# A decode block whose 26 large loads are issued by GpSimd in place of the sync engine

## The chip, the cores and the metric

The kernel runs on one core of a Trainium2 chip. A core has a matrix engine (TensorE, PE in the profile, its weight loads PEld), a vector engine (VectorE, DVE), a scalar engine (ScalarE, ACT), a general engine (GpSimd, POOL) and a sync engine (SyncE, SP). Each runs its own list of instructions in order and waits on semaphores for the others. Data come from memory by DMA: an engine issues a load, and 16 DMA engines carry it. In this kernel SP and ACT issue loads. The metric is device time in microseconds, the median of several runs.

## The reference

One decode step of a transformer block for a batch of 2 with one token each, hidden size 512. All is float32.

```
mod = silu(c) @ w_mod                        # 512 x 3072, cut into sa, ca, ga, sb, cb, gb
h   = layernorm(x) * (1 + ca) + sa
x   = x + ga * attention(h)                  # 32 query heads, 8 key heads, head size 128
h   = layernorm(x) * (1 + cb) + sb
x   = x + gb * (silu(h @ w1) @ w2)           # 512 x 1792 and back
```

The attention computes `q = h @ wq`, takes the last 4096 keys and values of the caches for each of the two tokens and the 8 key heads, and ends with `@ wo`. The caches' windows are 67 MB of the 97.5 MB that have to be read; w_mod, wq, wo, w1 and w2 are the rest. Every byte is used once.

## The kernel before

**The ring.** All large loads go into one buffer, `slots`, of 8 slots of 16 KB a partition. `stream(n)` hands out the next n slots in turn. `load_pair` (L77) loads the keys or the values of two heads of one token, 4096 KB, into two slots; `load_runs` (L88) loads a weight or a part of one. These two functions issue all 26 large loads, in program order: w_mod (three slots), wq (four slots), then for the eight steps of the attention K of the next step and V of the last one (16 loads), wo in two parts, w1 in two, w2 in four. A load into a slot waits until what stood there has been used. K of step 0 and K of step 1 take slots 0 to 3 after w_mod; V of step 0 takes slots 4 and 5 after wq.

**The start.** c is fetched by four small loads that ACT issues (L105), x by one that SP issues (L109). POOL makes the constants: a zeroed square and a diagonal (`ident`), then, from it by DVE, `id4` (L116) and other sums over `ident`, and from those on POOL `rep4` (L125), `selh`, `quad` (four selects, L185), `mix`, `selg`, a row of small memsets, and the memsets of `qg` and `qbd` (L210), `oTn` (L214), `hT` (L292) and `uT` (L293). DVE turns c (`cT`, L255) and, with ACT, makes silu of it (`scT`, L261). PE multiplies `scT` with w_mod in four rounds of four matmuls each into `m_a` (two of the six parts of mod, L269) and `m_sp` (the other four, L272). For the layer norm of x two small matmuls average statistics (`mean_a`, L236; `var_a`, L245); ACT takes a square root (L247). From `m_a` and the normalised x come `h_a` and its turned form `hq_T`. ACT copies `m_sp` to `mod_sp` (L286); one is added to one part of it (L287); three parts are turned (`gaT`, `sbT`, `cbT`, L255).

**The query.** PE computes q (L302) from wq and `hq_T`. `place(n)` spreads each half: DVE turns it (L315), four copies of 32 partitions bring it into `qg` (L319), a matmul with `rep4` repeats it (L323), four copies make `qbd` (L329). `place(0)` stands before the attention, `place(1)` in its third step.

**The attention.** In each of eight steps DVE turns the keys (`keys`, L361, eight transposes of 128 x 1024), PE computes scores (L374), DVE and PE find maxima, ACT takes the exponentials (L406), the result is turned and spread (`turn`, L418 to L435), and PE multiplies by the values (`weighted`, L448). Then come wo, the second layer norm, w1, silu and w2; `busy(n)` adds matmuls whose result is not used. The output is stored by a DMA from SP (L704).

**Order.** Inside the attention and behind it most instructions are kept in program order by hand (`inorder`). In the start they are not: the framework's scheduler orders each engine's list, by when it estimates that an instruction can run. Where an instruction moves to another engine, or a load to another queue, the lists of the start can come out in another order, also for instructions that the diff does not touch.

Of the kernel before, what the change touches and what calls it, by code (L numbers as in the profile page):

```python
# [10 lines left out]
ALU = mybir.AluOpType  # L11
# [12 lines left out]
def adaln_block(  # L24
# [19 lines left out]
    nc = tc.nc  # L44
# [16 lines left out]
    def const(shape, name):  # L61
        return consts.tile(shape, F32, name=name)

    def bank(tag, name):
        return (psum1 if tag in "CO" else psum).tile([P, 512], F32, tag=tag, name=name)
# [4 lines left out]
    def stream(n=1):  # L70
        i = turn_of[0]
        if n % 2 == 0:
            i += -i % n
        turn_of[0] = i + n
        return slots[:, i % RING : i % RING + n, :].rearrange("p s e -> p (s e)")

    def load_pair(cache, s):  # L77


        i, b = divmod(s, B)  # L80
        t = stream(2)
        nc.sync.dma_start(
            t,
            cache[b, 2 * i : 2 * i + 2, SK - W :, :].rearrange("e (u n) d -> u e (n d)", u=P // 2),
        )
        return t

    def load_runs(w, per, lo, hi):  # L88

        e = w.shape[1]  # L90
        n = -(-(hi - lo) * e // 4096)
        t = stream(n)[:, : (hi - lo) * e].rearrange("p (q e) -> p q e", e=e)
        nc.sync.dma_start(t, w.rearrange("(p q) e -> p q e", q=per)[:, lo:hi, :])
        return t


# [2 lines left out]
    x_sp, c_sp = xc[:, 0, :], xc[:, 1, :]  # L99
    nc.vector.memset(xc, 0.0)  # L100
    wm = load_runs(w_mod, 4, 0, 4)
    rows8 = lambda t: t.rearrange("(ab r) m -> ab r m", r=16)[:, 0, :]
    for b in range(B):
        for lo in (0, 2):
# [3 lines left out]
            )  # L108
    nc.sync.dma_start(rows8(x_sp), x2.rearrange("b (g m) -> g b m", m=P))  # L109
    wqt = load_runs(wq, 4, 0, 4)  # L110


# [103 lines left out]
    mod_sp = const([P, 4, P], "mod_sp")  # L216
# [36 lines left out]
    def turned(t, name):  # L253
        o = const([P, 4, 32], name)
        nc.vector.transpose(o, t.rearrange("p (m k) -> p k m", k=4))  # L255
        return o
# [7 lines left out]
    for k in range(4):  # L264
# [8 lines left out]
        if k == 0:  # L273
# [3 lines left out]
                xn, x_sp, mean_a, rstd_a, op0=ALU.subtract, op1=ALU.mult  # L277
# [6 lines left out]
    nc.vector.tensor_add(h_a, h_a, mod_a[:, 0, :])  # L284
    hq_T = turned(h_a, "hq_T")
    nc.scalar.copy(mod_sp.rearrange("p s m -> p (s m)"), m_sp)  # L286
    nc.gpsimd.tensor_scalar(mod_sp[:, 2, :], mod_sp[:, 2, :], 1.0, None, op0=ALU.add)  # L287
    ga, sb, cb1, gb = (mod_sp[:, s, :] for s in range(4))


    hT, uT = const([P, 4, 32], "hT_b"), const([P, F // P, 32], "uT")
# [18 lines left out]
    inorder = tc.keep_in_program_order  # L310

    def place(n):

        qT = once.tile([P, D], F32, tag="wide", name=f"qT{n}").rearrange("p (s j r) -> p s j r", s=4, r=32)
        inorder(nc.vector.transpose(qT.rearrange("p s j r -> p (s j r)"), q_ps[n]))  # L315
        for g in range(G):
            r = slice(32 * g, 32 * g + 32)
            eng = nc.gpsimd if g % 2 else nc.vector
            inorder(eng.tensor_copy(  # L319
                qg[n][r, :, :, :, g], qT[r, :, :, 0:32:16].rearrange("p s j b -> p s b j")  # L320
            ))
        rp = bank("C", f"qr{n}")[:, :P]
        inorder(nc.tensor.matmul(  # L323
            rp, rep4, qg[n].rearrange("p s b j g -> p (s b j g)"), start=True, stop=True
        ))
        for i in range(4):
            r = slice(32 * i, 32 * i + 32)
            cp = nc.scalar.copy if i % 2 else nc.vector.tensor_copy
            inorder(cp(  # L329
                qbd[n][r].rearrange("p s b j c -> p (s b j) c")[:, :, 4 * i : 4 * i + 4],  # L330
                rp[r, :].rearrange("p (m g) -> p m g", g=G),
            ))

    place(0)


# [12 lines left out]
    def fetch(s):  # L349

        if s < STEPS:
            kt[s] = load_pair(k_cache, s)
        if s > 0:
            vt[s - 1] = load_pair(v_cache, s - 1)
# [122 lines left out]
    for s in range(STEPS + 1):  # L477
        if s < STEPS:
            fetch(s + 1)
            scores(s, 0)  # L480
        if s > 0 and s != STEPS - 1:
            turn(s - 1)
        if s > 1:
            collect(s - 2)
        if s == 2:
            place(1)
        if s < STEPS:
            for j in range(1, 4):
                keys(s, j)
                scores(s, j)  # L490
            maxima(s)
            exponentials(s)
        if s < STEPS - 2:
            keys(s + 1, 0)
        if s > 0:
            weighted(s - 1)
        if s == STEPS - 2:
            turn(s)
            keys(s + 1, 0)
    collect(STEPS - 1)  # L500

    gaT, sbT, cbT = turned(ga, "gaT"), turned(sb, "sbT"), turned(cb1, "cbT")
    nc.gpsimd.tensor_copy(hT[:, :, 1:32:16], sbT[:, :, 0:32:16])
    ax = once.tile([P, P], F32, tag="ax", name="ax")
    for lo, hi in ((0, 24), (24, 32)):
        wt = load_runs(wo, 32, lo, hi)
        wot.extend(wt[:, q, :] for q in range(hi - lo))
# [69 lines left out]
    for q in range(28):  # L577
        g = q % 4
# [68 lines left out]
    for b in range(B):  # L647
# [5 lines left out]
            op0=ALU.mult,  # L653
# [5 lines left out]
    for tt in range(WIDE):  # L659
        g = tt % 4  # L660
# [21 lines left out]
    for tt in range(11, T2):  # L682
        for h in range(2):
            for g in range(4):
                lo = g * P + h * H
# [46 lines left out]
```

## Time and profile before

| | |
|---|---|
| median of 3 runs | 235.51 us (235.45 to 235.78) |
| profiled execution, first to last instruction | 233.7 us |
| PE busy | 161.1 us, 69% |
| DVE busy | 115.6 us, 49% |
| ACT busy | 28.5 us, 12% |
| POOL busy | 10.5 us, 4%, 35 instructions |
| read from memory | 97.53 MB, 417 GB/s over the span |

The profiled execution shows its span, 233.7 us; the time of a run is measured around it, and the median is 1.8 us longer. In the lines of the profile an engine's row reads: start, length, engine, line, operation, output and input, and in brackets how long the engine was idle before and what ended that. SPq and ACTq are the lists from which SP and ACT issue loads; the length of such a row is the issue, not the transfer. A row's `x8` is a number of instructions merged into one row.

### The profile page before, as it was taken

To read this page: it belongs to the slowest core of one execution; us is meant where nothing else is said; L and a number is where in the kernel's file an instruction comes from. 1 tells how busy PE (TensorE), PEld (TensorE's weight loads), DVE (VectorE), ACT (ScalarE), POOL (GpSimd) and SP (SyncE) were. 2 spreads that over 40 slices of the span, in tenths; PEclk is the share of its full clock that TensorE was granted. 3 is DMA by queue.
4 is the path that set the end of the run, shared out by engine and by line. 5 is a ranking of instruction groups with operands and counts; after the bars stand their busy time and mean duration, and the time that the engine had idled before them with its cause. 6 is when DMAs were issued, how large, how long until landed. Compare 5 with 4: busy or idle time off the path is not lost.

```text
span 233.7 us, 2571 instructions
## 1 busy us (share of the span) xinstructions
PE 161.1 (69%) x1070; PEld 43.3 (19%) x1070; DVE 115.6 (49%) x179; ACT 28.5 (12%) x64; POOL 10.5 (4%) x35
## 2 busy tenths in 40 slices
PE   0004916859577839797598749759759779789684
PEld 0001401201111111211120201202112122324222
DVE  0007240278894758695197089259559540101232
ACT  2000210000311120120210201111020120102020
POOL 2004710000000000000000000000000000000000
PEclk9999985979999977999979999988997997999999
DMA  7998998999999999999999999999999999989991
GB/s 269 446 542 359 404 494 359 446 444 421 415 421 449 446 437 415 426 426 446 449 437 409 418 437 449 449 421 412 426 444 449 443 421 437 463 367 437 424 404 57
DMA packets 3794, 97.68 MB, mean 418 GB/s; under 512 B 432, under 2 KB 456, under 8 KB 968
## 3 DMA queue, kind: packets, MB, share of 16 engines
q1 hardware_dynamic: 3768, 97.53, 97.1%
q8 instruction: 8, 0.13, 0.2%
q14 instruction: 2, 0.02, 0.0%
q10 hardware_dynamic: 16, 0.00, 0.0%
HBM read 97.53 MB, written 0.00 MB: 417 GB/s over the span
## 4 chain that ended last, share of the span: by engine, by line
DMA 60%; issue 18%; DVE 14%; PE 6%; POOL 0%; SPq 0%; POOLq 0%; ACT 0%
DMA slots<-in_A_k_cache_dram 22%; DMA slots<-in_A_wq_dram 15%; DMA slots<-in_A_v_cache_dram 12%; DMA slots<-in_B_w_dram 12%; DVE kT L361 11%; PE o L448 2%; PE q L302 2%; DVE zp L420 1%; PE acc_yw L661 1%; DVE xp L418 1%; PE qr L323 0%; PE acc_y L671 0%; DVE qT L315 0%; POOL qg L319 0%; SPq L109 0%
## 5 line engine op out<-in xcount | busy, mean ns | idle before, releaser
L361 DVE STREAM_TRANSPOSE kT<-slots 128x1024 f32<-128x1024 f32 x64 | 73.7, 1212 | 23.7 <-DMA slots<-in_A_k_cache_dram 23.6
L374 PE MATMUL s<-kT,qbd 128*32 128x512 f32 x256 | 68.6, 693 | 19.1 <-DVE kT L361 18.0
L448 PE MATMUL o<-slots,ptb 128*32 128x512 f32 x256 | 30.8, 624 | 2.1 <-DMA slots<-in_A_v_cache_dram 2.1
L374 PEld LDWEIGHTS s<-kT,qbd 128*32 128x32 f32 x256 | 9.6, 113 | 68.4 <-DVE kT L361 63.4
L269 PE MATMUL m_a<-slots,scT 128*32 128x256 f32 x32 | 4.4, 506 | 20.5 <-DVE scT L261 20.5
L302 PE MATMUL q<-slots,hq_T 128*32 128x512 f32 x64 | 8.3, 680 | 7.0 <-DMA slots<-in_A_wq_dram 7.0
L448 PEld LDWEIGHTS o<-slots,ptb 128*32 128x32 f32 x256 | 8.1, 114 | 17.9 <-issue 17.8
L404 ACT COPY bias<-bp 128x1 f32<-128x1 f32 x8 | 1.3, 159 | 77.0 <-PE bp L402 77.0
L384 DVE TENSOR_REDUCE mx<-s 128x1 f32<-128x512 f32 x8 | 5.5, 691 | 9.6 <-PE s L374 9.6
L565 PE MATMUL junk<-quad,id 128*32 128x512 f32 x22 | 10.2, 595 | 0.0
L420 DVE TENSOR_TENSOR zp<-xp,quarter 128x1024 f32<-128x1024 f32 x8 | 9.8, 1225 | 0.2
L435 ACT ACTIVATE ptb<-pT,odd 128x256 f32<-128x256 f32 x16 | 6.7, 472 | 25.6 <-PE pT L427 25.6
L255 DVE STREAM_TRANSPOSE cT<-xc 128x128 f32<-128x128 f32 x1 | 0.4, 401 | 16.7 <-DMA xc<-in_c_dram 16.7
L427 PE MATMUL pT<-zp,mix 128*32 128x256 f32 x64 | 5.7, 428 | 3.6 <-DVE zp L420 3.5
L458 ACT COPY ob<-o 128x512 f32<-128x512 f32 x8 | 4.7, 585 | 26.1 <-PE o L448 26.1
L272 PE MATMUL m_sp<-slots,scT 128*32 128x512 f32 x32 | 7.4, 738 | 0.0
L386 PE MATMUL mT<-ident,mx 128*1 128x128 f32 x16 | 3.0, 270 | 6.3 <-DVE mx L384 6.3
L315 DVE STREAM_TRANSPOSE qT<-q 128x512 f32<-128x512 f32 x2 | 1.4, 717 | 11.7 <-PE q L302 10.2
L418 DVE STREAM_TRANSPOSE xp<-pr 128x512 f32<-128x512 f32 x8 | 5.5, 686 | 3.4 <-ACT pr L406 3.4
L579 PE MATMUL acc_o<-slots,oTn 128*32 128x512 f32 x56 | 6.2, 593 | 0.7 <-DMA slots<-in_A_wo_dram 0.7
L466 PE MATMUL o_all<-ob,selh 128*64 128x128 f32 x64 | 6.0, 316 | 0.8 <-ACT ob L458 0.8
L550 DVE COPY acc_o_sb<-acc_o 128x256 f32<-128x256 f32 x1 | 0.4, 425 | 12.4 <-ACT acc_o_sb L549 12.4
(140 smaller groups left out, 93.8 us busy)
## 6 DMA issues: line engine op xcount, KB each, us to landing
slots<-in_A_k_cache_dram SPq DMA_DIRECT2D x8, 4096.0 KB, 27.4
slots<-in_A_v_cache_dram SPq DMA_DIRECT2D x8, 4096.0 KB, 27.6
slots<-in_w_mod_dram SPq DMA_DIRECT2D x1, 6144.0 KB, 17.1
slots<-in_A_wo_dram SPq DMA_DIRECT2D x1, 6144.0 KB
slots<-in_B_w_dram SPq DMA_DIRECT2D x1, 2688.0 KB
slots<-in_A_wo_dram SPq DMA_DIRECT2D x1, 2048.0 KB, 29.5
slots<-in_B_w_dram SPq DMA_DIRECT2D x1, 2048.0 KB
slots<-in_B_w_dram SPq DMA_DIRECT2D x1, 896.0 KB
```

Source lines behind the costliest of these rows:

```text
L272: nc.tensor.matmul(m_sp[r, :], scT[:, k, :], cd[:, g], start=(k == 0), stop=(k == 3))
L302: nc.tensor.matmul(q_ps[n][32 * g : 32 * g + 32, :], hq_T[:, k, :], wv[:, n, g], start=(k == 0), stop=(k == 3),)
L361: inorder(nc.vector.transpose(kT[s, j][:, 32 * c : 32 * c + 32, :], kt[s].rearrange("p (n j r) -> p j n r", j=4, r=32)[:, j, 32 * c : 32 * ...
L374: inorder(nc.tensor.matmul(s_ps[s][r : r + 32, :], qbd[h // 4][:, h % 4, b, j, :], kT[s, j][:, 32 * c : 32 * c + 32, e:32:2], start=(j == ...
L418: inorder(nc.vector.transpose(xp, pr[s]))
L420: inorder(nc.vector.tensor_mul(zp, xp[:, None, :, 0:16].to_broadcast([P, 4, 16, 16]), quarter[:, :, None, None].to_broadcast([P, 4, 16, 16 ...
L427: inorder(nc.tensor.matmul(tp[32 * i : 32 * i + 32, :], mix.rearrange("p v e -> p (v e)"), zp.rearrange("p y t x -> p (y t) x")[:, :, 4 * ...
L435: inorder(nc.scalar.activation(ptb[s % 2][:, :, e, :], tp.rearrange("p (w z) -> p w z", z=16), AF.Copy, scale=odd[:, e : e + 1],))
L448: inorder(nc.tensor.matmul(o_ps[s][r : r + 32, :], ptb[s % 2][:, w].rearrange("p e z -> p (e z)"), vt[s].rearrange("p (c w m f d) -> p c f ...
L466: inorder(nc.tensor.matmul(o_all[r : r + 64, :], selh[:, m, lo : lo + 2 * HQ], o_sb[s][:, m * DH : (m + 1) * DH], start=(s == 0 and m < 2) ...
L565: inorder(nc.tensor.matmul(junk[0:32, :], id4, quad.rearrange("p m y -> p (m y)"), start=True, stop=True,))
L579: inorder(nc.tensor.matmul(acc[32 * g : 32 * g + 32, :], oTn[:, q, :], wot[q], start=(q < 4), stop=(q >= 24),))
```

## The change

`load_pair` and `load_runs` issue from GpSimd. The add of one (L287) goes from GpSimd to VectorE; in `place` every second copy into `qg` goes from GpSimd to ScalarE (four in all, two for each half); the copy of `sbT` into `hT` (L503) goes from GpSimd to ScalarE. The loads of x and c and the store of the output stay where they are.

```diff
@@ load_pair
-        nc.sync.dma_start(
+        nc.gpsimd.dma_start(
             t,
             cache[b, 2 * i : 2 * i + 2, SK - W :, :].rearrange("e (u n) d -> u e (n d)", u=P // 2),
         )
@@ load_runs
-        nc.sync.dma_start(t, w.rearrange("(p q) e -> p q e", q=per)[:, lo:hi, :])
+        nc.gpsimd.dma_start(t, w.rearrange("(p q) e -> p q e", q=per)[:, lo:hi, :])
@@ adaln_block
     nc.scalar.copy(mod_sp.rearrange("p s m -> p (s m)"), m_sp)
-    nc.gpsimd.tensor_scalar(mod_sp[:, 2, :], mod_sp[:, 2, :], 1.0, None, op0=ALU.add)
+    nc.vector.tensor_scalar(mod_sp[:, 2, :], mod_sp[:, 2, :], 1.0, None, op0=ALU.add)
@@ place
-            eng = nc.gpsimd if g % 2 else nc.vector
-            inorder(eng.tensor_copy(
+            cp = nc.scalar.copy if g % 2 else nc.vector.tensor_copy
+            inorder(cp(
                 qg[n][r, :, :, :, g], qT[r, :, :, 0:32:16].rearrange("p s j b -> p s b j")
             ))
@@ adaln_block
-    nc.gpsimd.tensor_copy(hT[:, :, 1:32:16], sbT[:, :, 0:32:16])
+    nc.scalar.copy(hT[:, :, 1:32:16], sbT[:, :, 0:32:16])
```

POOL's list then holds its constants and the 26 loads: w_mod and wq ahead of the constants, the two first K loads behind the last memset (L293), and all other loads behind those.

## The prediction

> **What bounds the kernel now.** I read the page's slices and queues first, then the loads (their issues and landings), then stretches of time by windows, then the start of the run instruction by instruction.
>
> ```profile
> span 233.7 us, 2571 instructions
> ...
> DMA  7998998999999999999999999999999999989991
> ...
> q1 hardware_dynamic: 3768, 97.53, 97.1%
> ```
>
> The sync engine's queue q1 keeps 16 DMA engines busy for 97.1% of the span; no other engine comes near that. The windows (span of time, its length, busy time of PE, PEld, DVE, ACT, POOL, granted clock, DMA share, GB/s) say the same for the stream:
>
> ```profile
> 2.00:18.00 16.00, 0.00 (x0) 0.00 (x0) 0.12 (x1) 1.28 (x1) 0.22 (x1) 1.00 1.01 432
> 18.00:37.00 19.00, 9.81 (x68) 3.34 (x68) 7.96 (x31) 2.44 (x4) 7.94 (x23) 0.90 0.96 414
> 37.00:225.00 188.00, 146.62 (x905) 37.72 (x906) 105.08 (x139) 24.43 (x58) 0.97 (x4) 0.93 1.00 431
> ```
>
> From 2 to 225 us the share is 0.96 to 1.01 at 414 to 432 GB/s. A stream with no hole cannot absorb one: a microsecond in which no load is queued is a microsecond at the end. The loads of the start, with the next ones, and the times from issue to landing:
>
> ```profile
> 0.73 0.38 SPq L93 DMA_DIRECT2D slots<-in_w_mod_dram  x1
> ...
> 1.93 0.58 SPq L93 DMA_DIRECT2D slots<-in_A_wq_dram  x1
> 29.08 1.84 SPq L82 DMA_DIRECT2D slots<-in_A_k_cache_dram  x2
> 43.97 0.54 SPq L82 DMA_DIRECT2D slots<-in_A_v_cache_dram  x1
> ```
>
> ```profile
> slots<-in_A_k_cache_dram SPq DMA_DIRECT2D x8, 4096.0 KB, 27.4
> slots<-in_A_v_cache_dram SPq DMA_DIRECT2D x8, 4096.0 KB, 27.6
> slots<-in_w_mod_dram SPq DMA_DIRECT2D x1, 6144.0 KB, 17.1
> ...
> xc<-in_c_dram ACTq DMA_DIRECT2D x4, 1.0 KB
> ...
> slots<-in_A_wq_dram SPq DMA_DIRECT2D x1, 35.2
> ```
>
> A cache load of 4096 KB needs 9.7 us at 431 GB/s and lands 27.4 after its issue, so 17.7 us of other loads stand ahead of it. The place where little is queued is the start: w_mod and wq are all there is until the first two K loads, issued at 29.08, some 7.5 us before the wq data end. Where that is, the finer windows show:
>
> ```profile
> 1.00:1.50 0.50, 0.00 (x0) 0.00 (x0) 0.13 (x1) 0.00 (x0) 0.42 (x2) 1.00 0.00 0
> 1.50:2.00 0.50, 0.00 (x0) 0.00 (x0) 0.00 (x0) 0.00 (x0) 0.50 (x2) 1.00 2.98 885
> ...
> 36.00:36.25 0.25, 0.00 (x0) 0.00 (x0) 0.00 (x0) 0.00 (x0) 0.00 (x0) 0.50 0.00 0
> 36.25:36.50 0.25, 0.00 (x0) 0.00 (x0) 0.00 (x0) 0.00 (x0) 0.00 (x0) 0.50 1.22 524
> 36.50:36.75 0.25, 0.00 (x0) 0.00 (x0) 0.00 (x0) 0.00 (x0) 0.00 (x0) 0.50 3.36 1442
> ```
>
> A packet is counted where it starts, so shares above 1 are engines starting long packets together. The first w_mod packets start in 1.5 to 2.0, about 1.1 us behind the issue at 0.73. The engines turn from wq to the K packets at about 36.6.
>
> **The change, part by part.** Everything hangs on when GpSimd (POOL) reaches the first K load. SP had nothing else to do; POOL runs in order, and as built the two K loads stand behind its whole preparation of constants, from L125 to the memset at L293. The rows of that road, as they run now:
>
> ```profile
> 1.16 2.62 ACTq L105 DMA_DIRECT2D xc<-in_c_dram  x4
> 17.88 0.40 DVE L255 STREAM_TRANSPOSE cT<-xc 128x128 f32<-128x128 f32 x1 [16.75 <-DMA xc<-in_c_dram]
> 20.37 0.37 DVE L116 TENSOR_REDUCE id<-ident 128x32 f32<-128x128 f32 x1
> 20.51 1.08 PE L269 MATMUL m_a<-slots,scT 128*32 128x256 f32 x8 [20.51 <-DVE scT L261]
> 20.80 0.29 POOL L125 COPY rep<-id 128x128 f32<-128x128 f32 x1 [18.58 <-DVE id L116]
> 23.23 0.59 PE L236 MATMUL mean_a<-mv_a,avg 128*128 128x1 f32 x2
> 26.37 0.38 PE L245 MATMUL var_a<-dm_a,avg 128*128 128x1 f32 x2
> 27.55 0.46 POOL L293 MEMSET uT<- 128x448 f32 x1
> 29.73 0.28 DVE L281 TENSOR_SCALAR mod_a<-m_a 128x128 f32<-128x128 f32 x1
> 30.38 0.59 ACT L286 COPY mod_sp<-m_sp 128x512 f32<-128x512 f32 x1 [1.98 <-PE m_sp L272]
> 31.02 0.38 DVE L255 STREAM_TRANSPOSE gaT<-mod_sp 128x128 f32<-128x128 f32 x1
> 31.05 0.53 POOL L287 TENSOR_SCALAR mod_sp<-mod_sp 128x128 f32<-128x128 f32 x1 [3.04 <-ACT mod_sp L286]
> 31.32 0.36 DVE L255 STREAM_TRANSPOSE sbT<-mod_sp 128x128 f32<-128x128 f32 x1
> 31.62 0.40 DVE L255 STREAM_TRANSPOSE cbT<-mod_sp 128x128 f32<-128x128 f32 x1
> ```
>
> Today POOL has its constants done at 28.01 (27.55 + 0.46), because DVE makes id4 (L116) at 20.37, right behind scT. Left there, POOL would issue K as early as SP does. But with the loads on POOL the scheduler orders DVE's start anew, as built: x's statistics, c's silu, then both mod_a lines, L287, the three transposes gaT, sbT, cbT, and only then L116. So id4, and with it all of POOL's preparation, waits for the whole w_mod product and for ACT's copy of it. On PE the two statistics matmuls move behind all of m_a and m_sp.
>
> *The late road.* From the first m_a matmul (20.51) to ACT's copy (30.38) are 9.87 us; mean_a and var_a leave the middle of it (0.59 and 0.38, partly covered: I take off 0.7), so 9.2. ACT's copy with its hand-over, 30.38 to 31.02, 0.64. On DVE L287 costs as L281 does, 0.28 against POOL's 0.53; with three transposes 0.3 apart and the last one's 0.40, L116 starts 1.25 later. L116 to POOL's start, 20.37 to 20.80, 0.43. POOL's preparation, 20.80 to 28.01, 7.2. Together 18.7 us from the first m_a matmul to the K issue.
>
> *The start of it.* POOL issues w_mod at 0.73 as SP did, as its first instruction behind the same barrier. What a load issued from POOL costs above one from SP no row shows. Call it d: at least 0 (the same engines carry it), at most the 1.84 us that the two K issues take on SP; I take 0.6, nearest to POOL's own instructions of ordinary size (0.29, 0.46, 0.53). By the Trainium skill, "DMA: Bandwidth & Descriptors", Specifications, the first byte comes after about 1 us from GpSimd and about 0.6 from sync or scalar; by those figures d is 0.4 and the forecast 238.2, an estimate; this trace has 1.1 for SP.
>
> w_mod then lands at 0.73 + 17.1 + 0.6 = 18.4. c is the other input of m_a. Its four small loads stay on ACT, issued from 1.16 on, yet land only when w_mod does, at 17.88: they take turns with w_mod's rows, one row of 48 KB on 16 engines being 1.8 us at 432 GB/s. The first c load should reach the engines at 1.16 + 1.1 = 2.3, w_mod now at 0.73 + 1.1 + 0.6 = 2.4: I take it that c gains one turn and lands 1.8 before w_mod, at 16.6. From c to the first m_a matmul are 2.63 (17.88 to 20.51): 19.3, later than w_mod's landing, so this decides.
>
> *The sum.* K is issued at 19.3 + 18.7 = 38.0; its packets start 1.1 + 0.6 later, 39.7. The wq data, behind w_mod without a gap, end at 36.6 + 0.6 = 37.2. The engines stand still for 2.5 us; the stream runs 3.1 us late in all (39.7 - 36.6).
>
> *What does not count.* First the rows:
>
> ```profile
> 22.04 0.28 DVE L231 BATCH_NORM_STATS2 st_a<-xc 128x6 f32<-128x128 f32 x1
> 26.84 1.28 ACT L247 ACT_TABLE_LOAD   x1 [7.96 <-PE var_a L245]
> 37.29 8.34 PE L302 MATMUL q<-slots,hq_T 128*32 128x512 f32 x64 [6.97 <-DMA slots<-in_A_wq_dram]
> 83.64 0.53 POOL L319 COPY qg<-qT 32x32 f32<-32x32 f32 x2 [40.02 <-DVE qT L315]
> 198.74 27.57 DMA slots<-in_B_w_dram
> ```
>
> The q product (L302) needs wq, which will land at 1.93 + 35.2 + 0.6 = 37.7, and hq_T. Behind L116 (30.4) DVE has 1.7 us of reductions (20.37 to 22.04), then mean and variance with PE, ACT's table load of 1.28 and six short operations: I estimate hq_T at 36.5. If it came 2 us late, V0, which q's end releases (43.97 now), would still have the two K loads, 19.4 us, queued ahead. On ACT the copy of sbT (L503) now stands ahead of the first pair of qg copies and waits for POOL's memset of hT, until about 38; q's product ends some 4 us later, so nobody waits for it. The qg pairs (0.53 on POOL) go to ACT at a like price; the second, at 83.64, has the full queue behind it. Without that cover each pair would cost 0.5. The other 22 loads are issued by a POOL that has nothing else left, and a cache load may go out late by 17.7 us before an engine misses it. The end is such a load too: the chain's last long step is a 27.57 us wait for w2.
>
> So the span goes from 233.7 to 236.8. The median of the three runs, 235.51, is 1.8 above the span; I keep that: **238.6 us**, 1.3% slower.
>
> **The rivals.**
>
> *c as late as before.* If d is small and c gains no turn, m_a starts at 20.51 + 0.6 = 21.1, K goes out at 39.8, packets at 41.5: late by 4.9, 240.4. For it: 2.3 against 2.4 is near a tie. Against: c is issued at the same time and w_mod only later. If c gains two turns or more, w_mod's landing decides, 18.6: late by 2.4, 237.9.
>
> *The hole is hidden.* POOL would have to issue K by 35.5. Then only the start's d is lost: 236.1, and 235.5 where d is nothing. Against: the order on POOL and DVE is fixed, and the 18.7 us consist of rows.
>
> *The engines do not take turns.* If w_mod from POOL runs on each engine as one piece, and wq as another, c's later loads come only behind wq, at 37.7; m_a at 40.4, K issued at 59.1, packets at 60.8: late by 24, 259.7. Against: c landed 19 us before wq although wq was queued from 1.93. But those were loads from SP. By the Trainium skill, same page, Queues, rings and completion order, an engine changes between queues at packet ends only, a packet being typically 9 to 17 descriptors; this case's 1.8 us turns do not agree with that for SP's loads, and no run yet shows POOL's.
>
> *A slower stream.* If loads from POOL leave a gap at each border, say 0.3 us over 24 loads, 7 us are added: 245.8. For it nothing is in the trace; against it the 17.7 us of queue.
>
> *A faster stream, the other side.* If the engines ran POOL's rows with less between them, the 97.53 MB could move quicker. They take 226 us now (97.53 MB at 431). To win back 3.1 the rate has to be 1.4% higher, 437 in place of 431; at 440 the time would be about 234. Against: no window above shows more than 432 over more than a microsecond.
>
> **How the numbers follow.** Forecast with c one or more turns ahead 0.50 (238.6), c late 0.23 (240.4), hidden 0.06 (236), no turns 0.09 (260), slower stream 0.08 (246), faster stream 0.04 (234). The range, 236.3 to 243.0, reaches from a hidden hole with its d to c late with d at its upper end (3.7 + 2 x 1.84 = 7.4 late); it leaves out about 0.2, mostly above. What differs by less than 0.2% (0.5 us) a measurement of this kernel can't tell from no change. Faster 0.03, same 0.03, slower 0.94: a hidden hole with a small d, or a stream that just makes up for the hole, is the same.
>
> **What would show it.** In the changed kernel the windows around 37 to 40 have a DMA share near 0, once; POOL waits for L116 until about 30, and its first K issue stands at about 38. c's wait on DVE ends before 17.9. Beyond 40 the share is 1.00 at 431 GB/s and the landing times stay at 27 us. Wrong would be: K issued before 36, or holes later on, or a window rate off 431 by more than 1%.

## The result and the profile after

The changed kernel takes 238.28 us (median of four runs, 238.03 to 238.54); the kernel before took 235.48 beside it. The ratio is 1.0115, with an interval of 1.0103 to 1.0126: 1.15% slower. 238.6 was forecast. The profiled execution has a span of 236.4 us, 1.9 below the median; the prediction's sum gave 236.8.

From the page of the changed kernel, the span, the DMA slices and the queue of the loads:

```profile
span 236.4 us, 2576 instructions
...
DMA  7999895999999999999999999999999999989991
...
q0 software_dynamic: 3680, 97.52, 96.3%
```

The loads have moved from q1 to q0. A DMA slice is the busy share, in tenths, of one of 40 equal parts of the span. Only the seventh is much changed, 8 before and 5 now; it covers 35 to 41 us. The windows (columns as in the prediction) show the start, this place, and the rest:

```profile
2.00:2.50 0.50, 0.00 (x0) 0.00 (x0) 0.00 (x0) 0.00 (x0) 0.50 (x2) 1.00 0.00 0
2.50:3.00 0.50, 0.00 (x0) 0.00 (x0) 0.00 (x0) 0.00 (x0) 0.50 (x2) 1.00 3.69 1083
...
36.50:37.00 0.50, 0.00 (x0) 0.00 (x0) 0.50 (x1) 0.20 (x1) 0.50 (x2) 0.50 0.00 0
37.00:37.50 0.50, 0.00 (x0) 0.00 (x0) 0.43 (x2) 0.00 (x0) 0.50 (x2) 0.50 0.01 0
37.50:38.00 0.50, 0.00 (x0) 0.00 (x0) 0.46 (x2) 0.00 (x0) 0.50 (x2) 0.50 0.01 0
38.00:38.50 0.50, 0.21 (x4) 0.21 (x8) 0.23 (x1) 0.00 (x0) 0.22 (x1) 0.50 2.05 590
...
40.00:225.00 185.00, 144.59 (x896) 36.66 (x889) 103.66 (x133) 24.80 (x61) 12.29 (x22) 0.90 1.00 432
```

Three things are to be seen. The first w_mod packets start in 2.5 to 3.0; before it was 1.5 to 2.0. From 36.5 to 38.0 no long packet starts. Part of that is no hole, since the last wq packets are still running: in the trace's packet records the last 16 packets of wq, one for each engine, end between 37.05 and 37.81 (mean 37.50) and the first 16 of K start between 38.31 and 38.87 (mean 38.53), so an engine stands still for 1.0 us on average. This is what is called the hole below. Before, both means were 36.57 and there was no hole. And from 40 us on the stream runs at 432 GB/s as it did.

The window that restarts the stream has one more thing in it: a share of 2.05 with 590 GB/s. In the steady stream a share of 1.00 goes with 432 GB/s, so 2.05 should carry 885. The packets of the restart take longer for the same bytes: the first 16 of K took 1.38 to 1.96 us, 1.71 on average, where the median of all K and V packets is 1.213. That is another 0.5 us.

The start, in order of time:

```profile
1.25 0.69 POOL L93 DMA_DIRECT2D slots<-in_w_mod_dram  x1 [0.80 <-POOLq L717]
...
16.80 0.40 DVE L255 STREAM_TRANSPOSE cT<-xc 128x128 f32<-128x128 f32 x1 [6.40 <-DMA xc<-in_c_dram]
19.43 1.08 PE L269 MATMUL m_a<-slots,scT 128*32 128x256 f32 x8 [19.43 <-DVE scT L261]
21.99 1.08 PE L269 MATMUL m_a<-slots,scT 128*32 128x256 f32 x8
24.55 1.03 PE L269 MATMUL m_a<-slots,scT 128*32 128x256 f32 x8
26.26 0.61 PE L269 MATMUL m_a<-slots,scT 128*32 128x256 f32 x8
27.80 0.59 ACT L286 COPY mod_sp<-m_sp 128x512 f32<-128x512 f32 x1 [10.00 <-PE m_sp L272]
29.46 0.32 DVE L116 TENSOR_REDUCE id<-ident 128x32 f32<-128x128 f32 x1
29.84 0.29 POOL L125 COPY rep<-id 128x128 f32<-128x128 f32 x1 [25.92 <-DVE id L116]
34.21 2.93 DVE L276 TENSOR_SCALAR xn_a<-xc,m_a,rs_a 128x128 f32<-128x128 f32 x1
36.60 0.46 POOL L293 MEMSET uT<- 128x448 f32 x1
37.02 1.21 POOL L82 DMA_DIRECT2D slots<-in_A_k_cache_dram  x2
37.83 0.40 DVE L255 STREAM_TRANSPOSE hq_T<-h_a 128x128 f32<-128x128 f32 x1
38.29 9.12 PE L302 MATMUL q<-slots,hq_T 128*32 128x512 f32 x64 [5.96 <-DVE hq_T L255]
```

This is the predicted road: `id4` (L116) at 29.46 in place of 20.37, POOL waiting 25.92 us for it, and the first K issue right behind POOL's last memset, at 37.02.

How late the stream is after the start can be read from one window over the first 79 us. Before and after, with the window that follows:

```profile
1.00:80.00 79.00, 43.25 (x252) 10.64 (x254) 35.03 (x64) 8.82 (x17) 9.55 (x28) 0.94 1.00 427
80.00:190.00 110.00, 84.45 (x510) 19.92 (x506) 73.36 (x85) 14.06 (x38) 0.49 (x2) 0.92 1.00 432
```

```profile
1.00:80.00 79.00, 42.35 (x242) 10.42 (x246) 35.20 (x63) 8.94 (x19) 13.34 (x33) 0.85 0.97 412
80.00:190.00 110.00, 84.20 (x498) 19.35 (x492) 74.04 (x85) 15.07 (x40) 6.81 (x12) 0.92 1.00 433
```

427 GB/s before, 412 after: 15 GB/s over 79 us, at 431 GB/s, are 2.7 us of stream (one GB/s is 0.18 us). A window counts a packet where it starts, so this is good to about 0.3 us. The packet records give it more closely, as the difference of the times by which both kernels have moved the same bytes: 0.95 while w_mod is loaded, 2.47 at 80 us, 2.51 at 223. So nothing of it comes back, and the steady stream adds nothing: the last step's keys start at 173.93 before and 176.44 after, 2.5 later. The store of the output is issued 2.7 later, so 0.2 to 0.3 come up at the very end. Rows of before, then of after:

```profile
77.15 2.37 DVE L361 STREAM_TRANSPOSE kT<-slots 128x1024 f32<-128x1024 f32 x2 [2.71 <-DMA slots<-in_A_k_cache_dram]
173.93 9.13 DVE L361 STREAM_TRANSPOSE kT<-slots 128x1024 f32<-128x1024 f32 x8 [2.12 <-DMA slots<-in_A_k_cache_dram]
231.07 0.64 SPq L704 DMA_DIRECT2D out_dram<-yo  x1
```

```profile
79.62 2.37 DVE L361 STREAM_TRANSPOSE kT<-slots 128x1024 f32<-128x1024 f32 x2 [2.77 <-DMA slots<-in_A_k_cache_dram]
176.44 9.13 DVE L361 STREAM_TRANSPOSE kT<-slots 128x1024 f32<-128x1024 f32 x8 [2.09 <-DMA slots<-in_A_k_cache_dram]
233.80 0.58 SPq L704 DMA_DIRECT2D out_dram<-yo  x1
```

So the reading to be tested: 0.9 us late at the first load, 1.0 of hole before the first K, 0.5 of slow restart, together 2.4 of the 2.5 by which the stream is late.

### The profile page after: what moved, and what is told of

Same layout as the page of the kernel before. It is cut to its first block, busy times and chain, and to the rows that moved or that the text cites. A ratio compares the mean times of both kernels' runs of the same rounds, so it can differ in the third digit from the quotient of the medians.

```text
span 236.4 us, 2576 instructions
## 1 busy us (share of the span) xinstructions
PE 162.5 (69%) x1070; PEld 43.1 (18%) x1070; DVE 118.2 (50%) x180; ACT 29.7 (13%) x69; POOL 23.5 (10%) x55
## 4 chain that ended last, share of the span: by engine, by line
DMA 47%; issue 33%; DVE 12%; POOL 5%; PE 1%; POOLq 0%; DVEq 0%
DMA slots<-in_A_k_cache_dram 29%; DVE kT L361 11%; DMA slots<-in_A_wo_dram 11%; DMA slots<-in_B_w_dram 7%; PE acc_o L579 1%; POOL slots L82 1%; POOL quad L185 1%; POOL qbd L210 1%; POOL slots L93 1%; DVE zp L420 1%; POOL oTn L214 0%; DVE xp L418 0%; POOL quad L183 0%; POOL selh L176 0%; POOL uT L293 0%
## 5 line engine op out<-in xcount | busy, mean ns | idle before, releaser
L374 PE MATMUL s<-kT,qbd 128*32 128x512 f32 x256 | 69.6, 734 | 19.2 <-DVE kT L361 18.4
L269 PE MATMUL m_a<-slots,scT 128*32 128x256 f32 x32 | 3.8, 565 | 19.4 <-DVE scT L261 19.4
L302 PE MATMUL q<-slots,hq_T 128*32 128x512 f32 x64 | 9.1, 733 | 6.0 <-DVE hq_T L255 6.0
L82 POOL DMA_DIRECT2D slots<-in_A_v_cache_dram x8 | 4.6, 575 | 62.8 <-PE o L448 31.3
L82 POOL DMA_DIRECT2D slots<-in_A_k_cache_dram x8 | 4.7, 582 | 59.9 <-DVE kT L361 58.8
L427 PE MATMUL pT<-zp,mix 128*32 128x256 f32 x64 | 6.2, 460 | 3.0 <-DVE zp L420 2.9
L272 PE MATMUL m_sp<-slots,scT 128*32 128x512 f32 x32 | 5.9, 827 | 0.0
## 6 DMA issues: line engine op xcount, KB each, us to landing
slots<-in_A_v_cache_dram POOLq DMA_DIRECT2D x8, 4096.0 KB, 28.4
slots<-in_w_mod_dram POOLq DMA_DIRECT2D x1, 6144.0 KB, 17.6
```

The costliest lines, as they stand in the source:

```text
L82: nc.gpsimd.dma_start(t, cache[b, 2 * i : 2 * i + 2, SK - W :, :].rearrange("e (u n) d -> u e (n d)", u=P // 2),)
L272: nc.tensor.matmul(m_sp[r, :], scT[:, k, :], cd[:, g], start=(k == 0), stop=(k == 3))
L302: nc.tensor.matmul(q_ps[n][32 * g : 32 * g + 32, :], hq_T[:, k, :], wv[:, n, g], start=(k == 0), stop=(k == 3),)
L374: inorder(nc.tensor.matmul(s_ps[s][r : r + 32, :], qbd[h // 4][:, h % 4, b, j, :], kT[s, j][:, 32 * c : 32 * c + 32, e:32:2], start=(j == ...
L427: inorder(nc.tensor.matmul(tp[32 * i : 32 * i + 32, :], mix.rearrange("p v e -> p (v e)"), zp.rearrange("p y t x -> p (y t) x")[:, :, 4 * ...
```

## The experiments

The theory (A): the loss is the late first load plus the hole with its restart, and a load is worth the same whoever issues it. The main rival (B): loads issued by POOL cost more in themselves, all along. A third (C): the four small operations on DVE and ACT cost something. Each run stands beside runs of the kernel before on the same chip (235.37 to 235.42).

**e1: the four small operations alone.** All loads stay on SP: against the changed kernel, in `load_pair` and `load_runs`:

```diff
-        nc.gpsimd.dma_start(
+        nc.sync.dma_start(
```

> All loads stay on SP, the four small operations move as in the change. Theory A (the 2.8 us are the late first load from POOL, the hole before the first K load and a little at the end): none of it is here, 235.5, within 0.3. Rival C (the operations moved to DVE and ACT sit on a path that counts): 236 or more. DVE's start keeps the order of the kernel before, L116 at about 20.4.

Measured: 235.43, ratio 1.0006 (0.9997 to 1.0014). The four small operations cost nothing; C falls.

**e2: w_mod and wq from SP, the other 24 loads from POOL.** Against the changed kernel, in `load_runs`:

```diff
-        nc.gpsimd.dma_start(t, w.rearrange("(p q) e -> p q e", q=per)[:, lo:hi, :])
+        (nc.sync if w is w_mod or w is wq else nc.gpsimd).dma_start(t, w.rearrange(...)[:, lo:hi, :])
```

> w_mod and wq from SP, the other 24 loads from POOL; POOL's constants then end at about 28 again, so that K is issued at about 29 to 30. Theory A: no late start and no hole, 235.5 to 235.9. Rival B (loads from POOL move slower in themselves, or leave gaps between loads): most of the 2.8 us stay, 237.5 or more.

Measured: 235.51, ratio 1.0007 (0.9997 to 1.0017). The scheduler leaves DVE's start as before, POOL gets its constants early and issues K from 28.79 on:

```profile
20.36 0.37 DVE L116 TENSOR_REDUCE id<-ident 128x32 f32<-128x128 f32 x1
28.79 0.74 POOL L82 DMA_DIRECT2D slots<-in_A_k_cache_dram  x1 [0.78 <-PE m_sp L272]
39.69 9.97 PE L302 MATMUL q<-slots,hq_T 128*32 128x512 f32 x64 [9.94 <-DMA slots<-in_A_wq_dram]
```

24 loads out of 26, 16 of them the caches, come from POOL and cost nothing. B falls for the whole steady part. The last row shows something else: K and wq now stand in two queues, the engines take turns between them, and q starts 2.4 us later than before (37.29). That costs nothing either. The order in which bytes come matters little here; only an engine that stands still counts.

**e6: only w_mod and wq from POOL.** The other half of e2; the small operations as in the change. In `load_pair`, then in `load_runs`:

```diff
-        nc.gpsimd.dma_start(
+        nc.sync.dma_start(
...
-        nc.gpsimd.dma_start(t, w.rearrange("(p q) e -> p q e", q=per)[:, lo:hi, :])
+        (nc.gpsimd if w is w_mod or w is wq else nc.sync).dma_start(t, w.rearrange(...)[:, lo:hi, :])
```

> Only w_mod and wq from POOL, the other 24 loads from SP; DVE's start in the order of the change, with L116 late. SP issues K as soon as m_sp ends. Theory A: only the late start, 236.3 (0.85 above before, as with id4 early). If the order of DVE's start cost time by itself (through hq_T and q): 236.8 or more.

Measured: 236.45, ratio 1.0042 (1.0029 to 1.0054): 1.03 us. Here `id4` is nearly as late as in the change (28.49), but SP issues K at 25.55 and no hole opens. What is left is the start.

```profile
25.55 1.84 SPq L82 DMA_DIRECT2D slots<-in_A_k_cache_dram  x2
28.49 0.33 DVE L116 TENSOR_REDUCE id<-ident 128x32 f32<-128x128 f32 x1
```

**e7: the change, with the first two K loads from SP.** In `load_pair`:

```diff
-        nc.gpsimd.dma_start(
+        eng = nc.sync if cache is k_cache and s < 2 else nc.gpsimd
+        eng.dma_start(
```

> As the change, but the first two K loads are issued by SP: POOL still makes its constants late, and only those two loads no longer wait for it. Theory A: no hole, 236.3. If the late constants hold up something else (qbd, qg, the first scores): more, up to 238.

Measured: 236.30, ratio 1.0043 (1.0026 to 1.0060): 0.88 us. Two loads moved back take away 1.3 to 1.9 us of the loss of 2.15 to 2.80 (the change in its two sessions). It is these two that POOL's late constants hold up.

**e3: the change, with `id4` early again.** All 26 loads stay on POOL. DVE's start is put in the order of before by keeping `id4`, three other small sums that come from `ident`, and c's transpose in program order; the three are marked like `id4`.

```diff
+    inorder = tc.keep_in_program_order
-    nc.vector.tensor_reduce(
+    inorder(nc.vector.tensor_reduce(
         id4, ident.rearrange("p (a r) -> p r a", r=32), axis=AX.X, op=ALU.add
-    )
+    ))
...
-        nc.vector.transpose(o, t.rearrange("p (m k) -> p k m", k=4))
+        turn_ = nc.vector.transpose(o, t.rearrange("p (m k) -> p k m", k=4))
+        if name == "cT":
+            inorder(turn_)
```

> All 26 loads from POOL as in the change, but id4 and the other sums over ident are kept ahead of c's silu on DVE, so that POOL's constants are ready early. Theory A: K is issued as soon as m_sp ends, about 28; the hole (1.4 us) is gone, the late start (0.95) and the end (0.35) stay: 236.8. xn_a on DVE takes 0.35 us again in place of 2.93, as POOL's memsets lie elsewhere. Rival B: 238.3 as the change.

Measured: 236.25, ratio 1.0040 (1.0026 to 1.0053): 0.84 us. From its start:

```profile
17.27 0.46 POOL L296 MEMSET uT<- 128x448 f32 x1
26.33 0.60 POOL L82 DMA_DIRECT2D slots<-in_A_k_cache_dram  x1 [8.60 <-PE m_sp L275]
```

POOL has all its constants by 17.7 and then waits for w_mod's slots, as SP did. With every load on POOL, and no hole, the loss is the same 0.84 to 1.03 as in e6 and e7. So the start is worth about 0.9 and the hole the rest; e3 takes the hole away without touching a load. The expectation was 0.55 too high, most of it the 0.35 that it gave to the end, which is not lost here.

**e5: the change again**, since the experiments ran at another time than the first measurement. No edit.

> The changed kernel once more, beside the others. Its first profile has a late start of 0.9, a hole that moved the stream another 1.45 and 0.35 at the very end, where the last w2 load landed 0.7 us behind its data. If the end belongs to loads from POOL: 238.3 and the same late landing. If the end was chance: 237.9 to 238.1 and a last landing as quick as before.

Measured: 237.57 (237.40 to 238.72), ratio 1.0104 (1.0082 to 1.0125): 2.15 us. The median is 0.7 below that of the first four runs; four of the six runs lie at 237.40 to 237.61 and two, 238.69 and 238.72, above all of the first four. The profile shows one cause of such differences. The start of this run:

```profile
19.44 1.08 PE L269 MATMUL m_a<-slots,scT 128*32 128x256 f32 x8 [19.44 <-DVE scT L261]
22.00 0.98 PE L269 MATMUL m_a<-slots,scT 128*32 128x256 f32 x8
23.67 0.60 PE L269 MATMUL m_a<-slots,scT 128*32 128x256 f32 x8
24.96 0.60 PE L269 MATMUL m_a<-slots,scT 128*32 128x256 f32 x8
26.50 0.59 ACT L286 COPY mod_sp<-m_sp 128x512 f32<-128x512 f32 x1 [8.69 <-PE m_sp L272]
35.72 1.21 POOL L82 DMA_DIRECT2D slots<-in_A_k_cache_dram  x2
```

The first m_a matmul starts at the same time (19.44 and 19.43), but PE goes over to short matmuls (0.60 for eight in place of 1.08) one round earlier, ACT's copy comes 1.30 earlier, and the K issue too (35.72, not 37.02). PE's rate decides how long the hole is, because the late road leads through the w_mod product. The question of the expectation is answered too: PE doesn't wait for the last w2 load here. Of the twelve profiles only the first of the change has that wait, though in seven w2 comes from POOL, so it was chance and not POOL's.

This profiled run was one of the long ones, span 236.9, in spite of its shorter hole. Its bytes are 2.0 late at 80 us (416 GB/s in that window), but the last step's keys are 3.6 late:

```profile
177.54 9.13 DVE L361 STREAM_TRANSPOSE kT<-slots 128x1024 f32<-128x1024 f32 x8 [2.17 <-DMA slots<-in_A_k_cache_dram]
```

The packet records say a part of why: the engines came back at 37.31 to 39.05, with first packets of up to 2.37 us. Each of the 16 engines reports when it is done with a load; from the first engine to the last these reports are 3.8 us apart for the first K load, and still 3.6 for the last V load, where two engines are 2 us behind the next. The kernel before has 1.9 for its first K load without any hole, and the first profile of the change 1.7, so an uneven restart is not shown to be all of it. The last V packet ends at 196.55 (195.52 in the first profile, 192.93 before). A load has landed when its slowest engine is done, so what holds up single engines costs more than its mean.

**e4: the change, with two memsets more** ahead of K, both of 128 x 1024 like the one they repeat (0.94 us).

```diff
-    nc.gpsimd.memset(oTn, 0.0)
+    for _ in range(3):
+        nc.gpsimd.memset(oTn, 0.0)
```

> The change, with the memset of oTn (0.94 us) done three times in place of once ahead of the first K load. Theory A: every microsecond on POOL ahead of K is one at the end, 238.3 + 1.9 = 240.2. If the hole were not what counts (the queue makes up for it later): 238.3.

Measured: 239.17, ratio 1.0159 (1.0145 to 1.0173). The expectation was 1.0 too high: the memsets added 1.9, but `id4` came 0.59 earlier in this run (28.87), by PE's rate again, and K was issued at 38.22, only 1.20 after the first profile's. The store of the output moved by 0.91 (234.71 against 233.80). The direction and about the size are A's: POOL's time ahead of K shows at the end.

**e8: the loads alone.** The four small operations stay on POOL; against the changed kernel:

```diff
-    nc.vector.tensor_scalar(mod_sp[:, 2, :], mod_sp[:, 2, :], 1.0, None, op0=ALU.add)
+    nc.gpsimd.tensor_scalar(mod_sp[:, 2, :], mod_sp[:, 2, :], 1.0, None, op0=ALU.add)
...
-            cp = nc.scalar.copy if g % 2 else nc.vector.tensor_copy
-            inorder(cp(
+            eng = nc.gpsimd if g % 2 else nc.vector
+            inorder(eng.tensor_copy(
...
-    nc.scalar.copy(hT[:, :, 1:32:16], sbT[:, :, 0:32:16])
+    nc.gpsimd.tensor_copy(hT[:, :, 1:32:16], sbT[:, :, 0:32:16])
```

> The 26 loads from POOL, the four small operations left on POOL. L287 (0.5 us) then stands among POOL's constants ahead of the first K load, DVE has L287 and cbT less ahead of L116 (0.5 us), and the second K load stands behind the first pair of qg copies. Theory A: the same hole within 0.3, and the second K load, issued about 45, still comes before the first one's data end at 48: 238.3. If moving the four operations is what keeps the loads going: 239 or more.

Measured: 238.39 (237.58 to 238.82), ratio 1.0121 (1.0102 to 1.0140). Within its scatter this is the change. What moves is the second K load, which now stands behind copies that wait for q:

```profile
36.15 0.63 POOL L82 DMA_DIRECT2D slots<-in_A_k_cache_dram  x1
45.55 0.52 POOL L319 COPY qg<-qT 32x32 f32<-32x32 f32 x2 [8.77 <-DVE qT L315]
46.06 0.57 POOL L82 DMA_DIRECT2D slots<-in_A_k_cache_dram  x1
```

The second K load's packets start from 47.7 on, when the first load's have just run out. There is hardly a hole, but the first packets take up to 2.1 us again: a second slow restart. By the bytes moved, the stream is 1.8 late at 45 us and 2.7 at 61. The first hole was smaller in this profile, since K was issued at 36.15 and not 37.02. Moving the copies off POOL avoids the second restart; what that is worth in time lies inside the scatter.

**e9 and e10: the hole made with SP.** If B is to fall for the hole too, SP's loads must pay the same for one. In the kernel before, POOL clears a piece of slot 0, nine times in e9 as shown and thirteen times in e10; K's load into slot 0 must wait for that, and it overwrites what was cleared.

```diff
     nc.gpsimd.memset(uT, 0.0)
+    for _ in range(9):
+        nc.gpsimd.memset(slots[:, 0, 0:1024], 0.0)
```

> The kernel before, with all loads on SP and the four operations on POOL; POOL clears 1024 elements of slot 0 nine times (0.94 us each) behind its constants, and the first K load, into that slot, waits for it until about 37. The hole of the change, without a load from POOL and without its late start. Theory A (the hole itself costs, whoever issues, with a slow restart of the engines of some 0.5 us): K's packets start at about 38, 1.4 late, and the time is 237.2 to 237.6. Rival B (what costs is that the loads come from POOL): 236.5 or less, the hole's 1.1 alone without the restart, or nothing.

> The same with thirteen clears in place of nine: the hole is 3.7 us longer. Theory A: 3.7 more than the kernel with nine clears, 241. If the queue of later loads could make up for a hole: less.

Measured: e9 238.53, ratio 1.0124 (1.0104 to 1.0145), 3.16 us over before. e10 242.77, ratio 1.0304 (1.0283 to 1.0326), 7.40 us. Rows of e9, then of e10:

```profile
37.27 1.25 SPq L82 DMA_DIRECT2D slots<-in_A_k_cache_dram  x2
36.50:38.50 2.00, 1.35 (x8) 0.46 (x12) 0.00 (x0) 0.00 (x0) 0.75 (x1) 0.50 0.03 8
38.50:39.00 0.50, 0.50 (x8) 0.17 (x4) 0.00 (x0) 0.00 (x0) 0.00 (x0) 0.50 2.73 786
```

```profile
41.30 1.25 SPq L82 DMA_DIRECT2D slots<-in_A_k_cache_dram  x2
36.50:42.50 6.00, 5.26 (x28) 1.50 (x32) 0.00 (x0) 0.00 (x0) 4.54 (x5) 0.55 0.02 3
42.50:43.00 0.50, 0.50 (x12) 0.17 (x8) 0.00 (x0) 0.00 (x0) 0.00 (x0) 1.00 2.19 655
```

No loads start for 2 us, then for 6. The restart is slow here as well (2.73 with 786 GB/s; first packets 1.78 us on average). In e9 wq ends at 36.50 on average and K starts at 38.86: a hole of 2.36, plus 0.57 of restart, makes 2.9; 3.16 were lost. e9 lost more than was expected, because K's packets started 0.9 later, on the mean, than the 38 from which the expectation was worked out: SP's load took 1.4 us from its issue to the first packet, where w_mod takes 1.0. From e9 to e10 K's issue moves by 4.03 and its packets by 4.1, and the time by 4.24. So a hole behind SP costs as much as one behind POOL, and each further microsecond is one at the end.

**All runs in one table.** Late at 80 us is worked out as above, first from the window 1 to 80 (427 GB/s in before), then from the bytes moved by the packet records; the store is the issue of the output's DMA against before's 231.07, in the same profile; the last column is the measured median less that of the runs beside it.

| kernel | 1 to 80, GB/s | late at 80 us, window | late at 80 us, bytes | store later by | time over before |
|---|---|---|---|---|---|
| e1, operations only | 427 | 0.0 | 0.02 | 0.06 | 0.02 |
| e2, start on SP | 426 | 0.2 | 0.00 | -0.07 | 0.10 |
| e3, `id4` early | 423 | 0.7 | 0.83 | 0.84 | 0.84 |
| e7, two K on SP | 424 | 0.5 | 0.85 | 0.75 | 0.88 |
| e6, start on POOL | 421 | 1.1 | 1.01 | 0.97 | 1.03 |
| e5, the change again | 416 | 2.0 | 1.94 | 3.31 | 2.15 |
| the change | 412 | 2.7 | 2.47 | 2.73 | 2.80 |
| e8, loads only | 411 | 2.9 | 2.70 | 3.08 | 2.97 |
| e9, hole with SP | 411 | 2.9 | 2.83 | 2.83 | 3.16 |
| e4, two memsets more | 406 | 3.8 | 3.68 | 3.64 | 3.76 |
| e10, longer hole | 391 | 6.6 | 6.83 | 6.96 | 7.40 |

The last four columns follow each other, those by bytes and by time most closely (within 0.35, but for e10); from 80 to 190 us every one of these kernels runs at 431 to 433 GB/s. What a kernel has not read by 80 us it pays at the end. None of the kernels is faster than the one before; e2 equals it, with 24 loads on POOL.

## Why the prediction was right, step by step

The forecast, 238.6, lies 0.3 above the first measurement and 1.0 above the second. Its mechanism was the right one. Its terms were off in both directions and partly made up for each other; that the time came out within 0.3 is in part luck.

*The stream has no hole and cannot absorb one: right.* The table shows it, e10 most plainly.

*`id4` slips behind the w_mod product and K behind POOL's constants: right.* L116 started at 29.46, forecast 30.4. e3, which changes only that order, takes the hole away.

*c gains one turn and lands at 16.6, m_a starts at 19.3: right.* 16.80 and 19.43. With it the rival "c as late as before" (240.4) falls, and so does "the engines do not take turns" (259.7): c landed 20.7 us before the wq data ended (16.80 and 37.50) although both weights were queued by POOL, and in e2 POOL's K took turns with SP's wq.

*d, 0.6 at each start: too small at the first load.* The term was taken to be only the way from issue to packet. It is two things. POOL issues w_mod at 1.25, not 0.73 (0.52 later; its row shows 0.80 of waiting on its own queue first), and its first packet starts 1.39 after the issue, against 1.03 for SP. Together 0.88, and on the mean of the 16 engines 0.89. In the kernel before, POOL began its list at 0.73, with a memset, so the 0.52 belong to its first load; what they consist of is open. The step "POOL issues w_mod at 0.73 as SP did" failed. By the Trainium skill, "DMA: Bandwidth & Descriptors", Specifications, the way to the first byte is about 0.4 longer from GpSimd; the 0.36 here agrees with that (0.31 of it is the issue itself, 0.69 us in place of 0.38), and the 0.52 come on top of it in this kernel. At the K load d was nothing: the first packet came 1.29 after POOL's issue, and 1.39 after SP's in e9. e3, e6 and e7 put the whole at 0.84 to 1.03 us of time. The upper bound of d was misread: the row of 1.84 us spans two issues of 0.53 to 0.60 us with a wait between them, and the upper end of the range, 243.0, rests on it.

*The late road, 18.7 us: it was 17.6.* Nearly all of that is PE. From the first m_a matmul to ACT's copy 9.2 were taken from the row of before; it was 8.37, and 7.06 in e5. POOL's preparation was 7.18 where 7.2 was said; ACT and DVE together were 0.3 shorter.

*K issued at 38.0, packets at 39.7, a hole of 2.5: the place was right, the size too big.* 37.02, 38.53 and 1.0. The issue was 1.0 earlier, the way to the packets 0.2 shorter, and wq ended 0.3 later because the start was later: 1.5 less in all.

*The engines start again at full speed: not said, but assumed, and wrong.* The restart adds 0.5, and another 0.3 comes up at the end, where in this profile the last w2 load was late for L686. So the sum of 3.1 became 0.95 of start (wq ended 0.94 later than before), 1.0 of hole, 0.5 and 0.3: about 2.7.

*What does not count: right in its result.* hq_T was estimated at 36.5 and stood at 37.83, ending at 38.23. The operations behind L116 were as quick as estimated but for one: `xn_a` took 2.93 us, not 0.35, while POOL ran its memsets. q started at 38.29, 0.6 after the landing that was forecast for wq (37.7); as the prediction said, the two K loads in the queue covered it. The small operations cost nothing (e1).

*The slower and the faster stream: both fell.* 432 GB/s after, 431 before. A cache load lands 26.0 to 28.4 us after its issue (medians of K and V), where 27 was said.

## What to carry to other kernels

Where one DMA queue carries a kernel without a hole, which engine issues a load matters little; what that engine has to do ahead of the load matters a lot. Before loads go to an engine that computes, write down what stands ahead of each of the first loads in its list, and what that waits for in turn; here it was a sum on another engine that the scheduler had put behind a matmul product, because the loads had changed engines. Price the start of the stream and every stop of it in full: the idle time, and a slow first packet on each engine, and the slowest of the 16.

## What the runs showed of the hardware that was not expected

*A stream that has stopped restarts slowly.* Behind every hole, SP's or POOL's, the first 16 packets of K took 1.64 to 1.84 us on average in place of 1.213, single ones 1.2 to 2.4. At the very start it is the same: the first 16 of w_mod, of 48 KB, took 2.45 us on average before and 2.52 after, in place of 1.815. In e5 the engines came back unevenly and did not even out: first and last were done 3.8 us apart with the first K load and 3.6 with the last V load. A hole need not do that: with the first K load it was 0.7 in e9 and 0.6 in e10, and 1.9 in the kernel before, which has no hole. Nor is it shown to be why runs of one kernel differ; the kernel before has a run a microsecond above its median too (236.52, median 235.37).

*DVE beside POOL's memsets.* `xn_a`, a tensor_scalar from on-chip memory (SBUF) to on-chip memory, of 0.35 us, took 2.93 in the changed kernel, 2.73 in e5 and 4.52 in e4, and ended within 0.1 of POOL's last memset each time (37.14 and 37.06; 35.85 and 35.76; 38.34 and 38.26). In e3, where POOL was done, it took 0.34. The Trainium skill, "SBUF — State Buffer", Who interferes with whom, says that such a DVE operation and one of GpSimd can lock each other out of a shared port for a whole instruction. The trace agrees that they collide, but the wait here lasted over several memsets. In these three runs the memsets follow each other without a gap, and `xn_a` ends 0.08 us behind the last. In e8 it took 2.17 and ended 0.08 behind the last memset ahead of an operation of another kind (35.20 and 35.12); in e10 it took 0.99, with a gap of 0.06 between the memsets, and ended 0.08 behind the one beside which it began (28.83 and 28.75). In e9 it took 0.34 as it does alone, but it began late in a memset and ended 0.09 behind it, so that run can't tell. All these rows fit a wait until POOL's row of memsets has a gap or ends; no run varied the gap alone.

*The pace of matmuls.* In all these starts m_a and m_sp run at half pace first, and then at full: eight matmuls in 1.08 us, then in 0.60. The switch came 6.0 us after the first matmul in the changed kernel (between the third round's m_a and m_sp) and 3.3 in e5. The granted clock in the rows of windows is 1.00 all through, but only because the trace has no clock record ahead of the switch and the view counts that time as 1.00: the first record, of 1.00, starts at 25.40 in the changed kernel and at 22.76 in e5, where the rows turn short. In the twelve traces it starts 3.3 to 6.0 us behind the first matmul, and every record but the last is a whole multiple of 3.41 us long. Between the two profiles of the change the switch came 2.65 us earlier and the K issue 1.30: a part of the hole that no edit set. By the Trainium skill, "TensorE: Matmul & The Clock Gate", Part 1: The HAM clock gate, PE runs at half its clock until it has been busy for about 3.4 us of a window that runs freely. The factor of two agrees, and so does the grid of 3.41 us. The Trainium skill also puts the switch at about 4 us there; e5's 3.3 is near that, the 6.0 is longer.
